# A list-scheduled plan that begins four experts earlier, with the sums of those experts' weights split ahead

## The chip, the cores and the metric

The kernel runs on one core of a Trainium2 chip, as one program of five engines (TensorE, VectorE, ScalarE, GpSimd and SyncE, in the profile PE, DVE, ACT, POOL and SP) that each run their own queue in order and wait for each other on semaphores. The metric is the device time of one execution in microseconds: the median of three runs was 1813.43 us (1811.5 to 1813.5).

## The reference

Four batches of 576 tokens and 8 heads of 64 go through a retention layer (attention scores times a decay, no softmax). The result is 2304 tokens of 512 values. A first mixture of experts sends each token through one of 8 experts, and a second one sends every token through all 8 and adds them with weights `P` from a Sinkhorn iteration:

```
logits = x @ w_gate;  P = exp(logits - logits.max())
for _ in range(8):
    P /= P.sum(1, keepdims=True) + 1e-09
    P /= P.sum(0, keepdims=True) + 1e-09
    P *= N / E
for e in range(E):
    h = np.maximum(x @ w1[e], 0.0)        # 2304x512 @ 512x1024
    out += P[:, e:e+1] * (h @ w2[e])      # 2304x1024 @ 1024x512
```

All is float32. The second mixture is most of the work.

## The kernel before

A float32 matrix is cut into a high half that TensorE takes (`fp32r`) and the rest (`lo_of`, line 236), and a product is three matmuls: high by high, high by low, low by high. ScalarE makes the high half, VectorE the low one.

After retention and the first mixture (from about 98 to 338 us) the second mixture goes over the tokens in 3 passes of 768, and in each pass over 8 experts. The first weights use a scheme of seven products instead of eight, on sums and differences of blocks. A unit is a quarter of an expert's hidden columns: 7 products of 6 matmuls with 384 columns each.

**The hand-written part** is pass 0, 32 units (`unit`, line 1243). Its raw weights come by DMA into 5 raw tiles, and each weight tile is made in four steps (`split_step`, line 239) into one of 4 ring tiles. A "plain" slot is split as it is. A "sums" slot first needs four additions of 128x256 on GpSimd into the one tile `sums`; steps 0 and 1 split loaded blocks, steps 2 and 3 the sums. The steps are dropped at fixed places of a unit: `mid` "a" to "d" and three places of their own. At its start a unit stores its finished sums to HBM (`w1s`), 896 KB for each half, so that the later passes need not make them again. Between its products a unit does the second weights' work of the unit before it in plain form (`second`, line 1179): 36 matmuls of 512 columns. In experts 0 and 1, `gate_step` (line 1326) also runs the Sinkhorn iteration at places "b" and "d", and at its end `weigh` (line 1212) multiplies the six accumulators by `P`, three of them on GpSimd.

**The plan** does passes 1 and 2. Each piece of work is a `Task` with an engine, a duration and what it comes after. TensorE's order is written out (`line0` for the plan's first expert, in which the last hand-written unit's second weights are finished, then `GAPS`); every other engine takes the ready task that is due first, in a simulated run. In the plan the second weights use the scheme of seven products too: 252 matmuls of 256 columns for an expert. Weight sums are read back from `w1s`. The step from one pass to the next is `load_pass` (line 1462).

Of the kernel before, what the change touches and what calls it, by code (L numbers as in the profile page):

```python
# [7 lines left out]
F32 = mybir.dt.float32  # L8
# [28 lines left out]
def kernel(  # L37
# [18 lines left out]
    nc = tc.nc  # L56
    N, DM = out.shape
    E, _, F = w11.shape
# [86 lines left out]
    NP = 3  # L145
    RING = 4
# [18 lines left out]
    SPOTS = "bd"  # L165
    raws, slots, lo_n = [], [], [LO_AT]
# [5 lines left out]
    class Slot:  # L172
        def __init__(self, kind, parts, col=0):
            self.kind, self.parts, self.col = kind, parts, col
            slots.append(self)
            for r in parts:
                raws[r][3] = len(slots)
# [17 lines left out]
    def w2_slots(i):  # L195
        for f in range(2):
            Slot("plain", [part((i, f, r), lambda i, f, r: rows2(expert(w12, i), 2 * f + r))
                           for r in range(2)])

    for i in range(E):  # L200
        w1_slots(i)
        w2_slots(i)
    for p in range(1):
        for e in range(E):
            for j in range(2):
                pr = [part((e, j, h), lambda e, j, h: w21[e][:, h * half + 256 * j:h * half + 256 * (j + 1)]
                           .rearrange("(k p) f -> p k f", p=128)) for h in range(2)]
                Slot("sums", pr, 0)
                Slot("sums", pr, 128)
                Slot("plain", [part((e, j, h), lambda e, j, h: rows2(w22[e], 2 * h + j)) for h in range(2)])  # L210
    n_load, n_split, n_rel, n_take, n_known = [0], [0], [0], [0], [0]
# [12 lines left out]
    def load_more():  # L224
        while n_load[0] < n_known[0]:
            n = n_load[0]
            if n >= RAW and raws[n - RAW][3] * 4 > n_split[0]:
                return
            key, make, _, _ = raws[n]
            ap = make(*key)  # L230
            t = raws[n][2] = rawt[n % RAW]
            raws[n].append(arrives(1.46))
            nc.sync.dma_start(out=t.rearrange("p (k f) -> p k f", f=ap.shape[2]), in_=ap)
            n_load[0] += 1
# [4 lines left out]
    def split_step(n=1, force=False):  # L239
        for _ in range(n):  # L240
            load_more()
            j, s = divmod(n_split[0], 4)
            if j >= min(len(slots), n_rel[0] + RING):
                return
# [7 lines left out]
            if s == 0:  # L252
                c.hi, c.lo = (ringt[j % RING][:, 2048 * n:2048 * (n + 1)] for n in range(2))
# [11 lines left out]
            else:  # L265
                fa, fb = (raws[r][2].rearrange("p (k f) -> p k f", k=4)[:, :, c.col:c.col + 128] for r in c.parts)
# [14 lines left out]
            n_split[0] += 1  # L281
        load_more()

# [3 lines left out]
    def take():  # L287
        j = n_take[0]
# [4 lines left out]
        n_take[0] += 1  # L293
        return slots[j]

    def release(n=1):
        n_rel[0] += n
# [945 lines left out]
    def unit(u, pre, mids):  # L1243
# [3 lines left out]
        for k, x in enumerate((w.hi, w.lo)):  # L1247
            nc.sync.dma_start(out=w1s[4 * u["e"] + u["i"]][:, k], in_=x[:, 0:1792].bitcast(F32))
        arrives(5.2)
# [14 lines left out]
        def renew(j):  # L1264

            if u["last"]:
                xsplit(j)
# [11 lines left out]
        renew(0)  # L1279
# [7 lines left out]
        renew(1)  # L1287
# [4 lines left out]
        renew(2)  # L1292
# [6 lines left out]
        renew(3)  # L1299
# [6 lines left out]
        renew(4)  # L1306
# [5 lines left out]
        renew(5)  # L1312
# [5 lines left out]
        renew(6)  # L1318
# [29 lines left out]
    n_unit = E * 4  # L1348
    for g in range(n_unit):
# [3 lines left out]
             "last": e == E - 1 and i == 3 and p + 1 < NP}  # L1353
# [4 lines left out]
        elif g == 1:  # L1358
            mids = {k: (lambda _, n=n: gate_step(5 + n)) for n, k in enumerate(("p0", "p1", "p2"))}
            for k in "bcd":  # L1360
                mids[k] = gate_step
        elif p == 0 and e < 2 and gate_queue:
            mids = {k: gate_step for k in SPOTS}
        elif p + 1 < NP and e == E - 3 and i == 3:
            mids = {k: (lambda b, n=n: xload(p + 1, n)) for n, k in enumerate("bc")}
        elif p + 1 < NP and e == E - 2 and i > 1:
            mids = {"b": lambda b, n=i - 2: xsums(n)}
# [72 lines left out]
    JORD = {s: (0, 1, 2, 5, 3, 4, 6) if s < n_exp - 1 else (0, 1, 5, 6, 2, 3, 4) for s in range(E, n_exp)}  # L1440
# [74 lines left out]
    for s in range(E, n_exp):  # L1515
# [3 lines left out]
        for i in range(4):  # L1519
# [9 lines left out]
            where = {"x": 2 * (i % 2) if s == E else 0, "y": 1, "y5": 3 if s == E and i else 1}  # L1529
# [45 lines left out]
            product(0, [prev["x"] if s > E else prev.get(i % 2), tail[-1] if s == E and i else None])  # L1575
# [10 lines left out]
            product(5, [a0 if s > E or i == 0 else prev["y5"]])  # L1586
# [6 lines left out]
            prev["y"], prev["y5"] = a0 if s == E and i else a1, a1  # L1593
            if s == E:
# [3 lines left out]
        if s == E:  # L1598
# [120 lines left out]
        for j in JORD[s]:  # L1719
            for kh in range(2):  # L1720
                for t in range(HB):
                    so, bo = sops[j, kh], bops[j, kh]
                    dep = [so[1], so[2], bo[1], bo[2]]
                    if kh == 0:
# [3 lines left out]
                        else:  # L1728
                            dep += [last_ev[back, t]] if s > E else early_banks
# [17 lines left out]
    for s in range(E + 1, n_exp + 1):  # L1747
# [220 lines left out]
```

## Time and profile before

| what | value |
|---|---|
| median of 3 runs | 1813.43 us |
| profiled execution | 1811.14 us |
| its span | 1809.4 us, granted clock 0.999 |
| TensorE matmul busy | 1785.6 us, 99% |
| VectorE, ScalarE, GpSimd busy | 69%, 49%, 23% |
| DMA | 325.29 MB, mean 180 GB/s |
| first product of pass 0, of the plan | 337.7 us, 841.7 us |

The share of busy time is an average over stages, and matmuls are pipelined, so what a stage is worth is read from the distance of two starts in it. Whether a wait counts is read from whether TensorE stood still for it.

### The profile page before, as it was taken

To read this page: it belongs to the slowest core of one execution; us is meant where nothing else is said; L and a number is where in the kernel's file an instruction comes from. 1 tells how busy PE (TensorE), PEld (TensorE's weight loads), DVE (VectorE), ACT (ScalarE), POOL (GpSimd) and SP (SyncE) were. 2 spreads that over 40 slices of the span, in tenths; PEclk is the share of its full clock that TensorE was granted. 3 is DMA by queue.
4 is the path that set the end of the run, shared out by engine and by line. 5 is a ranking of instruction groups with operands and counts; after the bars stand their busy time and mean duration, and the time that the engine had idled before them with its cause. 6 is when DMAs were issued, how large, how long until landed. Compare 5 with 4: busy or idle time off the path is not lost.

```text
span 1809.4 us, 32670 instructions
## 1 busy us (share of the span) xinstructions
PE 1785.6 (99%) x12398; PEld 1705.3 (94%) x12398; DVE 1244.2 (69%) x2205; ACT 891.4 (49%) x1718; POOL 409.4 (23%) x396
## 2 busy tenths in 40 slices
PE   8999999999999999999999999999999999999998
PEld 7889999998999999998999999999999999999997
DVE  6764666557555655664667787787877777777777
ACT  2454455534443333343565555555656555555553
POOL 4630121221321212213221111111222112111212
PEclk9999999999999999999999999999999999999999
DMA  9854655564545556545755556555555555555540
GB/s 325 298 196 158 213 184 190 186 217 155 197 176 192 192 192 227 185 164 188 234 155 169 158 163 191 166 163 153 150 182 181 162 164 153 177 160 156 155 129 36
DMA packets 190597, 325.29 MB, mean 180 GB/s; under 512 B 20551, under 2 KB 93400, under 8 KB 190429
## 3 DMA queue, kind: packets, MB, share of 16 engines
q1 hardware_dynamic: 187132, 312.89, 53.2%
q0 software_dynamic: 3136, 9.95, 1.6%
q8 instruction: 100, 1.64, 0.4%
q14 instruction: 69, 0.56, 0.1%
q10 hardware_dynamic: 160, 0.26, 0.0%
HBM read 248.26 MB, written 74.79 MB: 179 GB/s over the span
## 4 chain that ended last, share of the span: by engine, by line
PE 86%; DVE 3%; issue 2%; ACT 1%; POOL 0%; POOLq 0%; DVEq 0%; ACTq 0%
PE b L1543 8%; PE b L1545 8%; PE b L1544 8%; PE b L1692 8%; PE b L1691 8%; PE b L1690 8%; PE b L1190 5%; PE b L1192 5%; PE b L1191 5%; PE b L1260 4%; PE b L1261 4%; PE b L1262 4%; PE b L722 4%; PE b L724 3%; PE b L723 3%
## 5 line engine op out<-in xcount | busy, mean ns | idle before, releaser
L1691 PE MATMUL b<-wb,sq 128*128 128x256 f32 x1344 | 378.5, 282 | 1.1 <-DVE wb L237 1.1
L1690 PE MATMUL b<-wb,sq 128*128 128x256 f32 x1344 | 377.1, 281 | 0.9 <-DVE a L1712 0.9
L1692 PE MATMUL b<-wb,sq 128*128 128x256 f32 x1344 | 377.1, 281 | 0.4 <-DVE sq L237 0.4
L1691 PEld LDWEIGHTS b<-wb,sq 128*128 128x128 f32 x1344 | 254.0, 189 | 1.7 <-DVE wb L237 1.7
L1692 PEld LDWEIGHTS b<-wb,sq 128*128 128x128 f32 x1344 | 254.4, 189 | 0.6 <-DVE sq L237 0.6
L1690 PEld LDWEIGHTS b<-wb,sq 128*128 128x128 f32 x1344 | 252.9, 188 | 1.8 <-issue 1.3
L237 DVE TENSOR_TENSOR ring<-raw,ring 128x512 fp32r<-128x512 f32 (+1 forms) x256 | 192.5, 761 | 69.2 <-ACT ring L260 61.0
L237 DVE TENSOR_TENSOR sq<-hq,sq 128x768 fp32r<-128x768 f32 x167 | 168.8, 1015 | 68.3 <-ACT sq L1636 68.2
L1448 POOL TENSOR_TENSOR raw<-raw,raw 128x512 f32<-128x512 f32 x60 | 84.8, 1414 | 384.2 <-DVE wb L237 313.3
L1558 ACT ACTIVATE hq<-hq 128x384 f32<-128x384 f32 x144 | 75.6, 526 | 184.4 <-DVE hq L1555 183.7
L1543 PE MATMUL b<-ch,wa 128*128 128x384 f32 x448 | 151.4, 338 | 2.2 <-DVE hq L1555 1.6
L1260 PE MATMUL b<-ch,ring 128*128 128x384 f32 x448 | 152.5, 340 | 0.2
L1543 PE MATMUL b<-c,wa 128*128 128x384 f32 x448 | 151.2, 337 | 1.1 <-ACT u L1549 1.1
L1636 ACT CAST sq<-hq 128x768 fp32r<-128x768 f32 x167 | 137.6, 829 | 29.2 <-PE b L1691 24.5
L1545 PE MATMUL b<-ch,wa 128*128 128x384 f32 x448 | 150.6, 336 | 0.0
L1545 PE MATMUL b<-c,wa 128*128 128x384 f32 x448 | 150.6, 336 | 0.0
L1261 PE MATMUL b<-cl,ring 128*128 128x384 f32 x448 | 150.6, 336 | 0.0
L1262 PE MATMUL b<-ch,ring 128*128 128x384 f32 x448 | 150.6, 336 | 0.0
L1544 PE MATMUL b<-cl,wa 128*128 128x384 f32 x448 | 150.6, 336 | 0.0
L1544 PE MATMUL b<-c,wa 128*128 128x384 f32 x448 | 150.5, 336 | 0.0
L1190 PE MATMUL b<-ring,HH 128*128 128x512 f32 x384 | 149.8, 390 | 0.0
L1192 PE MATMUL b<-ring,HL 128*128 128x512 f32 x384 | 149.5, 389 | 0.0
(258 smaller groups left out, 4179.5 us busy)
## 6 DMA issues: line engine op xcount, KB each, us to landing
wa<-w1s SPq DMA_DIRECT2D x192, 512.0 KB, 4.2
raw<-in_moe_w_dram SPq DMA_DIRECT2D x128, 512.0 KB, 3.9
w1s<-ring SPq DMA_DIRECT2D x64, 896.0 KB, 5.9
raw<-in_moe_w_dram SPq DMA_DIRECT2D x106, 256.0 KB, 3.5
wa<-w1s SPq DMA_DIRECT2D x64, 256.0 KB
sums<-in_moe_w_dram SPq DMA_DIRECT2D x22, 256.0 KB, 3.2
xs<-x SPq DMA_DIRECT2D x19, 256.0 KB, 4.8
kT<-in_kT_dram SPq DMA_DIRECT2D x18, 256.0 KB, 4.0
```

The costliest lines, as they stand in the source:

```text
L237: eng.tensor_tensor(lo, x, hi.bitcast(F32), ALU.subtract)
L1190: nc.tensor.matmul(y[t], hh[:, s], w.hi[:, f0:f0 + 512], start=first, stop=False)
L1192: nc.tensor.matmul(y[t], hl[:, s], w.hi[:, f0:f0 + 512], start=False, stop=end)
L1260: nc.tensor.matmul(ps, a, xh[:, r, :], start=first and r == 0, stop=False, skip_group_check=True)
L1261: nc.tensor.matmul(ps, a, xl[:, r, :], start=False, stop=False, skip_group_check=True)
L1262: nc.tensor.matmul(ps, b, xh[:, r, :], start=False, stop=r == 1, skip_group_check=True)
L1543: nc.tensor.matmul(ps, a, xh[:, r, :], start=first, stop=False, skip_group_check=True)
L1544: nc.tensor.matmul(ps, a, xl_[:, r, :], start=False, stop=False, skip_group_check=True)
L1545: nc.tensor.matmul(ps, b, xh[:, r, :], start=False, stop=r == 1, skip_group_check=True)
L1690: nc.tensor.matmul(ps, hh[:, r, c], wh[:, r], start=st, stop=False, skip_group_check=True)
L1691: nc.tensor.matmul(ps, hh[:, r, c], wl[:, r], start=False, stop=False, skip_group_check=True)
L1692: nc.tensor.matmul(ps, hl[:, r, c], wh[:, r], start=False, stop=kh == 1 and r == 1, skip_group_check=True)
```

## The change

The plan begins at expert 4 of pass 0 (`S0 = 4`), after 16 hand-written units instead of 32. What the plan needs from HBM for experts 4 to 7, their 16 tiles of sums, is made ahead: an extra "sums" slot with a `store` number loads one 128-column block of each half (two DMAs into one raw tile), goes through the same four steps into a ring tile, is stored to `w1s`, and its ring tile is free at once. Six such slots stand in the first mixture (`MADE_IN`), ten in experts 0 to 3. Ring tiles are handed out by a list of free ones. The places in a unit call `keep_up`, which does two steps where the splits are behind. The last unit no longer prepares the next pass, so both changes of pass are the plan's.

```
+    S0 = 4
+    MADE_IN = (0, 1, 1, 1, 1, 1, 1, 0)
+    made = [(e, i) for e in range(S0, E) for i in range(4)]
+    def make_ahead():
+        e, i = made.pop(0)
...
+        def source(e, i, _):
+            return [w21[e][:, h * half + 128 * i:h * half + 128 * (i + 1)].rearrange("(k p) f -> p k f", p=128)
+                    for h in range(2)]
+        Slot("sums", [part((e, i, 0), source)], 0, store=4 * e + i)
     for i in range(E):
         w1_slots(i)
-        w2_slots(i)
+        for _ in range(MADE_IN[i]):
+            make_ahead()
+        for f in range(2):
+            w2_slot(i, f)
...
+    for e in range(S0):
+        for j in range(2):
+            pr = sum_parts(e, j)
+            for col in (0, 128):
+                if made and (j or e in (1, 2) and col):
+                    make_ahead()
+                Slot("sums", pr, col)
...
-            if j >= min(len(slots), n_rel[0] + RING):
+            if j >= len(slots) or (s == 0 and not ring_free):
                 return
...
+                c.ring = ring_free.pop(0)
...
             n_split[0] += 1
+            if s == 3 and c.store is not None:
+                store_sums(c, c.store)
+                ring_free.append(c.ring)
...
         def mid(k, free):
...
             if free is not None:
-                split_step()
+                keep_up()
...
-    n_unit = E * 4
+    n_unit = S0 * 4
...
-        elif p + 1 < NP and e == E - 3 and i == 3:
-            mids = {k: (lambda b, n=n: xload(p + 1, n)) for n, k in enumerate("bc")}
...
-    for s in range(E, n_exp):
+    for s in range(S0, n_exp):
```

ScalarE's queue where expert 0 ends and expert 1 begins. `ring` is a ring tile, `c` a kept product or a hidden sum, `HH` the hidden tile's high half, `b0` a PSUM bank. Before:

```order
L1238 COPY c_6525<-b0_6482 128x384 [waits PE_49]
L279 CAST ring2_80<-sums_84 128x512 [waits Pool_49]
L1238 COPY c_6554<-b0_6482 128x384 [waits PE_49,Activation_49]
L279 CAST ring2_80<-sums_84 128x512 [waits Pool_49]
L1233 ACTIVATE HH_111<-b0_6482 128x384 [waits PE_49,Activation_49]
L279 CAST ring3_71<-raw2_65 128x512 [waits DMAHW0_49]
L1228 ACTIVATE HH_111<-c_6588 128x384 [waits DVE_49,Activation_49]
L279 CAST ring3_71<-raw3_66 128x256
L1228 ACTIVATE HH_111<-c_6619 128x384 [waits DVE_49,Activation_49]
L279 CAST ring3_71<-sums_84 128x512 [waits Pool_49]
```

and now:

```order
L1278 COPY c_6656<-b0_6611 128x384 [waits PE_49,Activation_49]
L308 CAST ring2_80<-sums_84 128x512 [waits Pool_49]
L308 CAST ring0_78<-raw2_65 128x512 [waits DMAHW2_49,DMAHW1_49]
L1278 COPY c_6691<-b0_6611 128x384 [waits PE_49,Activation_49]
L308 CAST ring0_78<-raw2_65 128x256 [waits DMAHW2_49]
L308 CAST ring0_78<-sums_84 128x512 [waits Pool_49]
L1273 ACTIVATE HH_111<-b0_6611 128x384 [waits PE_49,Activation_49]
L308 CAST ring0_78<-sums_84 128x512 [waits Pool_49]
L1268 ACTIVATE HH_111<-c_6725 128x384 [waits DVE_49,Activation_49]
L308 CAST ring0_78<-raw0_63 128x512 [waits DMAHW7_49,Activation_49]
L1268 ACTIVATE HH_111<-c_6760 128x384 [waits DVE_49]
```

A whole made-ahead slot (`ring0`) now stands between the last step of one sums slot and the first of the next, the copy of its sums ahead of the activation `HH<-b0`; and the slot after it begins in the same `ring0` (lane DMAHW7 is that of the store).

ScalarE's queue in the fourth unit of expert 1. Before:

```order
L279 CAST ring0_78<-raw0_63 128x512 [waits DMAHW3_49]
L1228 ACTIVATE HH_111<-c_7096 128x384 [waits DVE_49,Activation_49]
L279 CAST ring0_78<-raw1_64 128x256 [waits DMAHW0_49]
L1238 COPY c_7108<-b0_7065 128x384 [waits PE_49,Activation_49]
L279 CAST ring0_78<-sums_84 128x512 [waits Pool_49]
L1238 COPY c_7127<-b0_7065 128x384 [waits PE_49,Activation_49]
```

and now:

```order
L308 CAST ring1_79<-raw1_64 128x512 [waits DMAHW3_49]
L308 CAST ring1_79<-raw2_65 128x256 [waits DMAHW4_49]
L1268 ACTIVATE HH_111<-c_7275 128x384 [waits DVE_49,Activation_49]
L308 CAST ring1_79<-sums_84 128x512 [waits Pool_49]
L1278 COPY c_7287<-b0_7242 128x384 [waits PE_49,Activation_49]
L308 CAST ring1_79<-sums_84 128x512 [waits Pool_49]
L308 CAST ring2_80<-raw3_66 128x512 [waits DMAHW6_49,DMAHW5_49]
L1278 COPY c_7312<-b0_7242 128x384 [waits PE_49,Activation_49]
```

The copy of the sums has moved ahead of the first kept product (`c_7287`), and a step of the next slot stands ahead of the second.

GpSimd's queue at the start of the plan (`out_0_dram` is a scatter of finished rows, `raw` the second weights' blocks). Before:

```order
L237 TENSOR_TENSOR cl_10152<-x_9126,ch_10151 128x768 [waits Activation_49]
L112 DMA out_0_dram<-a0_6673,idc_2052 2304x512 [waits DMAHW5_49,DVE_49]
...
L112 DMA out_0_dram<-a4_6747,idc_2052 2304x512 [waits DVE_49]
L1448 TENSOR_TENSOR raw3_66<-raw2_65 128x512 [waits DMAHW7_49,DMAHW6_49]
L1448 TENSOR_TENSOR raw2_65<-raw2_65,raw0_63 128x512 [waits DMAHW2_49,Pool_49]
...
L112 DMA out_0_dram<-a5_6752,idc_2052 2304x512 [waits DMASW7_49,DVE_49]
```

and now:

```order
L300 TENSOR_TENSOR sums_84<-raw1_64,sums_84 128x256 [waits Pool_49]
L1470 TENSOR_TENSOR raw3_66<-raw2_65 128x512 [waits DMAHW3_49,DMAHW2_49]
L1470 TENSOR_TENSOR raw2_65<-raw2_65,raw0_63 128x512 [waits DMAHW6_49,DMAHW5_49,Pool_49]
L1473 TENSOR_TENSOR raw0_63<-raw3_66,raw0_63 128x512 [waits DVE_49,Pool_49]
L1470 TENSOR_TENSOR raw1_64<-raw1_64,raw0_63 128x512 [waits DMAHW0_49,DVE_49,Pool_49]
```

The scatters, and the split `cl` of the next pass's tokens, no longer stand ahead of the plan's first sums.

## Rows read from the trace of the kernel before

**Rows 1.** Windows: PE, PEld, DVE, ACT, POOL busy us, granted clock, DMA share, GB/s.
```profile
594.00:656.00 62.00, 62.00 (x314) 56.16 (x313) 35.94 (x59) 24.69 (x52) 12.15 (x16) 1.00 0.52 187
941.00:1000.00 59.00, 59.00 (x423) 59.00 (x422) 45.05 (x70) 31.61 (x56) 10.37 (x8) 1.00 0.54 161
406.00:422.30 16.30, 16.21 (x83) 14.43 (x83) 13.28 (x32) 9.03 (x19) 3.63 (x4) 1.00 0.38 106
501.10:516.50 15.40, 15.40 (x79) 13.99 (x78) 8.64 (x14) 6.38 (x13) 3.20 (x4) 1.00 0.36 114
```

**Rows 2.** Timeline of PE: start us, duration; first matmuls of experts.
```profile
593.95 0.34 PE L1260 MATMUL b<-ch,ring 128*128 128x384 f32 x1
...
655.88 0.34 PE L1260 MATMUL b<-ch,ring 128*128 128x384 f32 x1
...
841.66 0.34 PE L1543 MATMUL b<-ch,wa 128*128 128x384 f32 x1
...
882.28 0.34 PE L1543 MATMUL b<-ch,wa 128*128 128x384 f32 x1
...
941.21 0.34 PE L1543 MATMUL b<-ch,wa 128*128 128x384 f32 x1
...
1000.15 0.34 PE L1543 MATMUL b<-ch,wa 128*128 128x384 f32 x1
...
1295.04 0.34 PE L1543 MATMUL b<-c,wa 128*128 128x384 f32 x1
...
1356.41 0.34 PE L1543 MATMUL b<-c,wa 128*128 128x384 f32 x1
```

**Rows 3.** Start of the plan: waits (total, times, longest us), then DVE and POOL timelines.
```profile
PE b L1543 <- DVE hq L1555: 1.6, 2, 1.0
...
859.01 3.10 DVE L237 TENSOR_TENSOR wb<-raw,wb 128x512 fp32r<-128x512 f32 x3
...
857.93 1.32 POOL L1448 TENSOR_TENSOR raw<-raw 128x512 f32<-128x512 f32 x1
```

**Rows 4.** Fourth unit of expert 0: timelines of DVE, POOL, ACT and PE.
```profile
399.88 1.29 DVE L237 TENSOR_TENSOR ring<-sums,ring 128x512 fp32r<-128x512 f32 x2
...
403.98 0.55 DVE L1226 TENSOR_TENSOR c<-b,c 128x384 f32<-128x384 f32 x1
...
401.25 0.74 POOL L272 TENSOR_TENSOR sums<-raw 128x256 f32<-128x256 f32 x1 [21.95 <-DVE ring L237]
...
401.86 0.49 ACT L1233 ACTIVATE HH<-b 128x384 fp32r<-128x384 f32 x1 [2.09 <-PE b L1262]
...
404.83 0.42 PE L1260 MATMUL b<-ch,ring 128*128 128x384 f32 x1
...
409.10 0.34 PE L1260 MATMUL b<-ch,ring 128*128 128x384 f32 x1
```

**Rows 5.** DMA, 607 to 617 us: GB/s in 40 slices; issues, KB, us to landing.
```profile
GB/s 33 0 0 0 0 41 49 147 180 279 295 225 254 279 438 496 446 430 459 459 459 430 430 402 315 430 401 401 459 459 459 229 86 0 0 0 0 0 0 0
...
w1s<-ring SPq DMA_DIRECT2D x2, 896.0 KB, 5.9
```

**Rows 6.** Fourth unit of expert 1: timelines of POOL, ACT and PE.
```profile
454.71 4.67 POOL L1218 TENSOR_SCALAR a<-a,P 128x512 f32<-128x512 f32 x3 [17.77 <-issue]
...
461.29 0.91 POOL L271 TENSOR_TENSOR sums<-raw,raw 128x256 f32<-128x256 f32 x1
...
460.33 0.47 ACT L1238 COPY c<-b 128x384 f32<-128x384 f32 x1
...
461.12 0.39 PE L1190 MATMUL b<-ring,HH 128*128 128x512 f32 x1
...
461.80 0.34 PE L1260 MATMUL b<-ch,ring 128*128 128x384 f32 x1
...
462.15 0.34 PE L1262 MATMUL b<-ch,ring 128*128 128x384 f32 x1
```

**Rows 7.** First mixture: timelines of DVE and POOL.
```profile
243.90 1.92 DVE L237 TENSOR_TENSOR ring<-raw,ring 128x512 fp32r<-128x512 f32 x1 [0.77 <-ACT ring L260]
...
243.43 1.83 POOL L237 TENSOR_TENSOR cl<-x,ch 128x768 fp32r<-128x768 f32 x1 [13.11 <-ACT ch L1075]
```

More of the change, by code (lines that the diff above doesn't have):

```diff
@@ L145 @@
     NP = 3
-    RING = 4
     GAT0 = 14
@@ L172, with __init__ @@
     class Slot:
-        def __init__(self, kind, parts, col=0):
-            self.kind, self.parts, self.col = kind, parts, col
+        def __init__(self, kind, parts, col=0, store=None):
+            self.kind, self.parts, self.col, self.store = kind, parts, col, store
+            self.ring = None
             slots.append(self)
@@ L252, in split_step @@
             if s == 0:
-                c.hi, c.lo = (ringt[j % RING][:, 2048 * n:2048 * (n + 1)] for n in range(2))
+                c.ring = ring_free.pop(0)
+                c.hi, c.lo = (ringt[c.ring][:, 2048 * n:2048 * (n + 1)] for n in range(2))
             if c.kind == "plain":
@@ L265, in split_step @@
             else:
-                fa, fb = (raws[r][2].rearrange("p (k f) -> p k f", k=4)[:, :, c.col:c.col + 128] for r in c.parts)
+                if c.store is None:
+                    fa, fb = (raws[r][2].rearrange("p (k f) -> p k f", k=4)[:, :, c.col:c.col + 128] for r in c.parts)
+                else:
+                    both = raws[c.parts[0]][2].rearrange("p (h k f) -> p h k f", h=2, k=4)
+                    fa, fb = (both[:, h] for h in range(2))
                 hi = c.hi.rearrange("p (j f) -> p j f", f=128)
@@ L281, in split_step, with store_sums @@
             n_split[0] += 1
+            if s == 3 and c.store is not None:
+                store_sums(c, c.store)
+                ring_free.append(c.ring)
         load_more()
+    def store_sums(c, n):
+        for k, x in enumerate((c.hi, c.lo)):
+            nc.sync.dma_start(out=w1s[n][:, k], in_=x[:, 0:1792].bitcast(F32))
+        arrives(5.2)
     def keep_up():
@@ L287, in take @@
     def take():
+        while slots[n_take[0]].store is not None:
+            n_take[0] += 1
         j = n_take[0]
@@ L293, in take, with release @@
         n_take[0] += 1
+        held.append(slots[j])
         return slots[j]
-    def release(n=1):
-        n_rel[0] += n
+    def release():
+        ring_free.append(held.pop(0).ring)
     tiles = _tiles()
@@ L1246, in unit @@
         w = take()
-        for k, x in enumerate((w.hi, w.lo)):
-            nc.sync.dma_start(out=w1s[4 * u["e"] + u["i"]][:, k], in_=x[:, 0:1792].bitcast(F32))
-        arrives(5.2)
+        store_sums(w, 4 * u["e"] + u["i"])
         if u["i"] % 2:
@@ L1311, in unit @@
         h_sum(u, 3, yb, u3)
-        renew(5)
         if pre:
@@ L1352 @@
         u = {"p": p, "e": e, "i": i, "h": {}, "y": {} if i == 0 else pre["y"], "w2": None,
-             "last": e == E - 1 and i == 3 and p + 1 < NP}
+             }
         mids = {}
@@ L1527 @@
             P_, made = {}, {}
-            where = {"x": 2 * (i % 2) if s == E else 0, "y": 1, "y5": 3 if s == E and i else 1}
+            where = {"x": 2 * (i % 2) if s == S0 else 0, "y": 1, "y5": 3 if s == S0 and i else 1}
             def chunk(j, wg=wg, bank_t=bank_t, where=where):
@@ L1746 @@
     b, owed = [], 0
-    for s in range(E + 1, n_exp + 1):
+    for s in range(S0 + 1, n_exp + 1):
         b += [g2[s - 1, j, kh, t] for j in JORD[s - 1] for kh in range(2) for t in range(HB)]
```

54 lines of the change are left out of this document (22 added, 32 removed).

## The prediction

> **What bounds the kernel now.** I read the windows of busy time first. An expert of the first pass's hand-written part and an expert of the plan both show TensorE busy in every microsecond, at a granted clock of 1.00 (the 2.4 GHz level), while VectorE is busy 35.9 of 62 us and 45.1 of 59 us, ScalarE 24.7 and 31.6 [rows 1]. So the time is the number of matmuls in each style, plus the places where TensorE waits. Next come the starts of experts on TensorE [rows 2]: two experts of the hand-written part start at 593.95 and 655.88, 61.93 us apart; two of the plan at 941.21 and 1000.15, 58.94 us apart. Both do 168 matmuls of 384 columns for the first weights; for the second weights the one does 144 of 512 columns, the other 252 of 256. Then I looked for what is not at this pace: the start of the plan, a pass change inside it, and the Sinkhorn steps in experts 0 and 1, where VectorE is busy 13.3 of 16.3 us against 8.6 of 15.4 in an ordinary unit [rows 1].
>
> **The change part by part.** The sum is made against the profiled execution: 1811.14 us, span 1809.4, and 2.3 us under the median of 1813.43.
>
> *Four experts move into the plan.* 4 x (61.93 - 58.94) = 12.0 us less [rows 2]. Nothing covers TensorE there, so this counts in full.
>
> *The start of the plan*, now after expert 3. Before, it takes from 841.66 to 882.28, 40.6 us [rows 2]. Its content is 168 matmuls of 384 columns, 0.174 us apart, and 36 of 512 columns, 0.227 us apart [rows 6], which is 29.2 + 8.2 = 37.4 us: 3.2 us are waits. Two of these waits, 1.6 us together, end with VectorE's addition for the hidden tile [rows 3]; VectorE is late because three weight subtractions took 3.10 us while GpSimd was doing its own sums [rows 3], against 0.65 us for such a subtraction alone (two in 1.29 us, [rows 4]). GpSimd does these sums late because scatters of the finished pass stand ahead of them in its queue. At expert 3 no pass ends, so the scatters are not there, and the sums can run earlier, beside idle stretches of VectorE. I take 0.8 us less; bounds: 1.6 us less if both waits go, 0.5 us more if the sums meet another VectorE operation.
>
> *A pass change inside the plan.* The change from pass 0 to pass 1 used to be made by hand in the last unit; it is now made by the plan, as the one from pass 1 to 2 is. That one takes 61.37 us from 1295.04 to 1356.41 [rows 2], 2.4 us over the pace. I add 2.4 us; bounds 1.5 and 4. Gain so far: 12.0 + 0.8 - 2.4 = 10.4 us.
>
> *Sixteen sums made ahead.* The work is the same as before for ScalarE, VectorE, GpSimd and the stores; it is moved from experts 4 to 7, six pieces into the first MoE and ten into experts 0 to 3 (2, 3, 3, 2). Each piece is 4 ScalarE copies, 4 VectorE subtractions, 4 GpSimd additions, two loads and two stores of 896 KB. On the average this fits: three pieces add some 3 x 4 x 0.65 = 7.8 us to VectorE's 36 of 62. What counts is the queues, since every engine runs in order. Where a critical operation must be done before TensorE's next product, a piece ahead of it can push it over. I went through the units in the changed order; three places are tight.
>
> First, the fourth unit of expert 0. Before, VectorE finishes the Sinkhorn step and then splits two pieces at 399.88 (1.29 us), GpSimd starts the next additions at 401.25, and ScalarE's activation comes at 401.86 [rows 4]. Now the last subtraction of one piece stands right before the first of a made-ahead piece, and there is one buffer for sums: GpSimd starts its additions at 400.6, three of them take 2.2 us (0.74 each), and ScalarE, whose copy of these sums now stands ahead of the activation, gets to it at 403.5 instead of 401.86. VectorE's subtractions and its addition follow (0.65, 0.55, 0.65 and 0.55 us): the addition ends at 406.0, where the one of before started at 403.98 and the product that needs it at 404.83 [rows 4]. Wait: 1.2 us.
>
> Second, the same ring buffer. This piece's store is issued at about 404.8 (high half) and 405.5 (low half), and the next piece takes the same buffer at once: ScalarE and VectorE wait for the store. A pair lands 5.9 us after its issue [rows 5]: 410.6. The queued subtraction (0.7) and the next addition (0.55) end at 411.9; the product that needs it starts at 409.10 before [rows 4], now 410.35: 1.5 us. ScalarE's copy for the product after that comes late too, by no more than it did before. The bounds of this store wait: nothing if the pair lands within 4.2 us, 2.6 us if other transfers stand before it. I take 1.4. Together 2.6 us.
>
> By the Trainium skill, DMA: Bandwidth & Descriptors, Specifications, one core has about 358 GB/s to HBM; the pair would then move for 5.1 us. The trace disagrees: slices of this stretch run at 430 to 459 GB/s [rows 5], and the pair moves in about 4.3 us. By the rule both store waits would be 0.8 us longer.
>
> Third, the second unit of expert 1 has the same two pieces back to back behind a Sinkhorn step: 1.2 us again, and its last Sinkhorn step is then late by 0.5 us: 1.7 us. Fourth unit of expert 1: GpSimd weights the accumulators for 4.67 us from 454.71, and the third addition after it ends at 462.2 [rows 6]. Before, ScalarE's copy for the next product stands ahead of the copy that waits for these sums, and is done at 460.8; the product starts at 461.80 [rows 6]. Now the order is the other way round: sums copy 462.25 to 462.87, then the 0.47 us copy, product at 463.3: 1.5 us. At the end of this unit the piece after the made-ahead one takes the same buffer again: 1.3 us more (I reckon 0 to 2.6 again). 2.8 us. Smaller shifts of VectorE in the other Sinkhorn units (a subtraction of 512 columns where one of 256 stood): 0.6 us. Bill of the hand-written part: 2.6 + 1.7 + 2.8 + 0.6 = 7.7 us; bounds 1 and 14.
>
> In the first MoE the six pieces fall into 16 slots per expert that had room: the second weights' part has only evictions to make, and three of the four doubled steps lie there. VectorE's subtractions are stretched where GpSimd works beside them: 1.92 us while GpSimd has one of 1.83 us [rows 7]. I take 0.3 us; bounds 0 and 9 (below).
>
> *Sum:* 1811.14 - 10.4 + 7.7 + 0.3 = 1808.7 for the profiled execution; with 2.3 us for the median, **1811.0 us**.
>
> **The rivals.** *The queues have the room* (28%). For it: everywhere outside the Sinkhorn units VectorE idles seven of 15.4 us [rows 1], and a delay of one operation in a unit need not reach TensorE. Against it: the buffer taken at once is there in the order, whatever the averages. If the store lands in time and the sums come early, some 1 to 2 us of the 8 remain: 1813.4 - 10.4 + 1.5 = 1804.5.
>
> *Slower: VectorE and GpSimd meet in the first MoE* (13%). If the additions of a made-ahead piece run in the first weights' part of an expert, beside the subtraction that frees a bank, each of the six pieces costs what the rows of one such meeting show: 1.92 - 0.65 = 1.3 us [rows 4, 7], and with the split that stands behind it some 1.7 us. Six times that is 10 us instead of 0.3: 1811 + 10 = 1821. It decides from 5.9 us of such waits on (the 2.4 us forecast and 3.6 more). Against it: the copies of a piece stand where the bank has no reader waiting, and its loads are issued well ahead, so that the additions run in the second weights' part.
>
> The Trainium skill, SBUF - State Buffer, "SBUF: two separate sides", says that GpSimd and a VectorE operation with two operands in SBUF exclude each other for a whole instruction. The trace agrees in kind (1.92 us here is 0.65 plus most of one GpSimd operation). By the rule each of the 64 GpSimd operations that are moved can hold VectorE for its whole 0.74 us; if one in four stands on the path, that is 12 us, which is this rival's size.
>
> *The plan does less than it says* (14%). If the start keeps its 3.2 us of waits and the pass change out of pass 0, with less lead for its loads, costs 4 us, the gain is 8 us, and the bill of 8 eats it: 1813.4, no change.
>
> **How the numbers follow.** Forecast 45%, with a range of its own from 1808.5 to 1813.5; the rivals 28, 13 and 14%. What can be told from no change is about 0.2%, 3.6 us: faster is under 1809.8, slower over 1817.0. Faster: all of the first rival and a third of the forecast, 0.43. Slower: 0.13. Between: 0.44. Range: 1803.5 (gain whole, almost no bill) to 1817.5, which leaves out most of the slow rival and a little at the fast end.
>
> **What would show it.** In the changed profile: experts 4 to 7 at 58.9 us each; a start of the plan of about 40 us and a pass change of about 61.4; on TensorE, waits of 1 to 2 us in the fourth units of experts 0 and 1 and the second of expert 1, put down to VectorE's hidden-tile addition or ScalarE's copy, and on ScalarE and VectorE behind them waits for a DMA at the ring's casts. No such waits would make the first rival right. Units of the first MoE longer by over 1 us each would make the second right. The forecast is wrong if experts 4 to 7 are not at the plan's pace, or if TensorE waits in experts 2 and 3, where I reckon with nothing.

## The result and the profile after

The changed kernel took 1828.0 us (median of 4 runs, 1824.6 to 1828.5), the kernel before 1813.5 beside it: 1.0078 times as long, 95% interval 1.006 to 1.0095. The forecast of 1811.0 and its range (to 1817.5) were wrong, and so was the sign; "slower" had 13%, for meetings in the first mixture that did not come. The profiled execution took 1827.6 us, span 1825.5.

First the starts of experts, PE's timeline of the changed kernel (start us, duration, in brackets the idle time before and what ended it); they answer to [rows 2].

```profile
342.19 0.34 PE L1298 MATMUL b<-ch,ring 128*128 128x384 f32 x1
...
617.68 0.69 PE L1565 MATMUL b<-ch,wa 128*128 128x384 f32 x1 [4.18 <-DMA wa<-w1s]
...
660.38 0.34 PE L1565 MATMUL b<-ch,wa 128*128 128x384 f32 x1
...
719.31 0.34 PE L1565 MATMUL b<-ch,wa 128*128 128x384 f32 x1
...
837.42 0.34 PE L1565 MATMUL b<-c,wa 128*128 128x384 f32 x1
...
898.78 0.34 PE L1565 MATMUL b<-c,wa 128*128 128x384 f32 x1
```

An expert of the plan takes 58.93 us (660.38 to 719.31), the change into pass 1 61.36: as forecast. Experts 0 to 3 took 275.5 us (342.19 to 617.68) where they took 256.25 before, and the plan starts with a wait of 4.18 us for its first weights. The windows of the changed kernel, in the columns of [rows 1], are an expert of the plan and the fourth units of experts 0 and 1:

```profile
660.40:719.30 58.90, 58.90 (x421) 58.90 (x420) 44.06 (x68) 30.27 (x54) 7.89 (x7) 1.00 0.63 197
...
468.30:487.80 19.50, 16.27 (x80) 13.83 (x79) 12.63 (x18) 10.38 (x21) 13.85 (x14) 1.00 0.61 222
396.60:416.10 19.50, 17.02 (x84) 14.32 (x83) 15.04 (x33) 8.69 (x19) 8.94 (x11) 1.00 0.61 235
```

TensorE is busy 16.3 and 17.0 of 19.5 us in these units, where [rows 1] has 16.2 of 16.3 in another unit with a Sinkhorn step, the first of expert 1. What it waits for, 345 to 490 us of the changed kernel (total, times, longest us):

```profile
PE b L1298 <- ACT c L1278: 4.2, 5, 2.2
PE b L1298 <- DVE c L1266: 3.6, 5, 1.3
PE b L1207 <- DVE HL L1274: 0.8, 2, 0.4
PE b L1298 <- DVE cr L1208: 0.6, 2, 0.3
```

These are the waits that the prediction named, for ScalarE's kept product and VectorE's hidden tile. The table has the us that each unit takes, from its first matmul on PE to the next unit's: before, after, and four of the experiments below. (0,3) is the fourth unit of expert 0.

| unit | before | after | e1 | e5 | e4 | e11 |
|---|---|---|---|---|---|---|
| (0,1) | 16.67 | 18.24 | 16.69 | 16.67 | 16.67 | 16.67 |
| (0,2) | 16.10 | 16.61 | 17.66 | 16.32 | 16.48 | 17.12 |
| (0,3) | 15.94 | 19.49 | 19.99 | 17.56 | 17.57 | 18.62 |
| (1,0) | 16.35 | 17.13 | 17.09 | 16.48 | 16.51 | 17.98 |
| (1,1) | 15.93 | 17.93 | 17.94 | 17.57 | 17.57 | 15.93 |
| (1,2) | 16.34 | 17.11 | 17.11 | 16.10 | 16.14 | 15.93 |
| (1,3) | 15.50 | 19.53 | 21.17 | 16.60 | 16.60 | 21.15 |
| (2,0) | 15.47 | 16.95 | 16.91 | 15.47 | 15.47 | 16.89 |
| (2,1) to (2,3) | 46.47 | 46.74 | 46.67 | 46.41 | 47.27 | 46.52 |
| (3,0) to (3,2) | 46.44 | 46.41 | 46.41 | 46.41 | 50.21 | 46.41 |
| (3,3) | 15.50 | 19.81 | 15.47 | 15.47 | 15.47 | 15.47 |
| plan's first expert | 40.62 | 42.70 | 40.59 | 40.97 | 40.32 | 40.31 |

The last matmul starts 16.1 us later than before, from these parts: the first unit starts 4.5 us later; units (0,1) to (3,2) take 14.9 more; (3,3), with the wait behind it, 4.3; the plan's first expert 2.1; the change into pass 1 2.7 (2.4 in its own expert, 0.25 in the one ahead of it); experts moved into the plan take off 12.0; 0.4 less elsewhere.

### The profile page after: what moved, and what is told of

Read it like the earlier page. It is cut to its first block, busy times and chain, and to the rows that moved or that the text cites. A ratio compares the mean times of both kernels' runs of the same rounds, so it can differ in the third digit from the quotient of the medians.

```text
span 1825.5 us, 34067 instructions
## 1 busy us (share of the span) xinstructions
PE 1782.6 (98%) x12830; PEld 1719.8 (94%) x12830; DVE 1323.2 (72%) x2320; ACT 949.0 (52%) x1798; POOL 455.9 (25%) x421
## 4 chain that ended last, share of the span: by engine, by line
PE 78%; DVE 5%; issue 4%; DMA 2%; POOL 1%; ACT 1%; POOLq 0%; SPq 0%; DVEq 0%; ACTq 0%
PE b L1565 10%; PE b L1567 10%; PE b L1566 10%; PE b L1714 10%; PE b L1713 10%; PE b L1712 10%; PE b L762 4%; PE b L764 3%; PE b L763 3%; PE b L1230 1%; PE b L1298 1%; PE b L1231 1%; PE b L1232 1%; PE b L1300 1%; PE b L1299 1%
## 5 line engine op out<-in xcount | busy, mean ns | idle before, releaser
L1713 PE MATMUL b<-wb,sq 128*128 128x256 f32 x1680 | 473.0, 282 | 1.1 <-DVE wb L261 1.1
L1714 PE MATMUL b<-wb,sq 128*128 128x256 f32 x1680 | 471.4, 281 | 0.8 <-DVE sq L261 0.8
L1712 PE MATMUL b<-wb,sq 128*128 128x256 f32 x1680 | 471.2, 280 | 0.9 <-DVE a L1734 0.9
L1714 PEld LDWEIGHTS b<-wb,sq 128*128 128x128 f32 x1680 | 318.0, 189 | 1.2 <-DVE sq L261 1.2
L1713 PEld LDWEIGHTS b<-wb,sq 128*128 128x128 f32 x1680 | 317.5, 189 | 1.7 <-DVE wb L261 1.7
L1712 PEld LDWEIGHTS b<-wb,sq 128*128 128x128 f32 x1680 | 316.1, 188 | 1.8 <-issue 1.3
L1565 PE MATMUL b<-c,wa 128*128 128x384 f32 x896 | 302.4, 337 | 2.0 <-ACT u L1571 2.0
L1567 PE MATMUL b<-c,wa 128*128 128x384 f32 x896 | 301.3, 336 | 0.0
L1566 PE MATMUL b<-c,wa 128*128 128x384 f32 x896 | 301.1, 336 | 0.0
L261 DVE TENSOR_TENSOR sq<-hq,sq 128x768 fp32r<-128x768 f32 x208 | 207.3, 1000 | 81.0 <-ACT sq L1658 80.9
L1734 DVE SCALAR_TENSOR_TENSOR a<-b,P,a 128x256 f32<-128x256 f32 x306 | 141.1, 476 | 49.7 <-PE b L1714 48.9
L261 DVE TENSOR_TENSOR wb<-raw,wb 128x512 fp32r<-128x512 f32 x231 | 163.1, 708 | 19.0 <-ACT wb L1658 19.0
L1565 PEld LDWEIGHTS b<-c,wa 128*128 128x128 f32 x896 | 169.1, 189 | 2.9 <-ACT u L1571 2.8
L1567 PEld LDWEIGHTS b<-c,wa 128*128 128x128 f32 x896 | 168.4, 188 | 0.0
L1566 PEld LDWEIGHTS b<-c,wa 128*128 128x128 f32 x896 | 168.3, 188 | 0.0
L1658 ACT CAST wb<-raw 128x512 fp32r<-128x512 f32 x231 | 142.6, 618 | 46.1 <-PE b L1714 44.5
L1571 ACT COPY u<-b 128x384 f32<-128x384 f32 x160 | 76.3, 477 | 74.1 <-PE b L1567 73.6
L285 ACT CAST ring<-raw 128x512 fp32r<-128x512 f32 x160 | 95.3, 619 | 9.0 <-DMA raw<-in_moe_w_dram 7.8
```

The lines of the kernel that those rows point to most:

```text
L261: eng.tensor_tensor(lo, x, hi.bitcast(F32), ALU.subtract)
L285: nc.scalar.copy(c.hi[:, o:o + 512], x[:, i:i + 512])
L1565: nc.tensor.matmul(ps, a, xh[:, r, :], start=first, stop=False, skip_group_check=True)
L1566: nc.tensor.matmul(ps, a, xl_[:, r, :], start=False, stop=False, skip_group_check=True)
L1567: nc.tensor.matmul(ps, b, xh[:, r, :], start=False, stop=r == 1, skip_group_check=True)
L1658: nc.scalar.copy(o.tile[0], src.tile)
```

## The experiments

In each the ratio is to the kernel before, run beside it (1810.9 us for e1 to e4, 1812.1 for e5 to e8, 1812.0 for e9 to e12).

### The place of the plan's first weights: e1

SyncE's timeline of the changed kernel shows the loads of these weights going out at 613.53 us, 4.2 us ahead of the matmul at 617.68; of SyncE's wait ahead of them, 14.2 us are put down to the last product of unit (3,3) (PE b L1300, last row: SyncE's waits, 594 to 620 us). The weights go into memory that had been a ring tile, and that tile was the one unit (3,3) was multiplying from.

```profile
591.94 1.05 SPq L318 DMA_DIRECT2D w1s<-ring  x2
613.53 3.25 SPq L1532 DMA_DIRECT2D wa<-w1s  x5
...
SPq L1532 <- PE b L1300: 14.2, 1, 14.2
```

```
-    ring_free, held = list(range(4)), []
+    ring_free, held = [0, 2, 1, 3], []
```

> The changed kernel (1828.0 us) with two of the four ring tiles exchanged (free list begins 0, 2, 1, 3 instead of 0, 1, 2, 3); nothing else differs. Theory, the place in memory: the plan's first weights are loaded into memory that the last hand-written unit still multiplies from, so their load is issued only at that unit's last product (613.5 us) and TensorE waits 4.2 us. With the exchange that ring tile is another one, the load goes out some 14 us earlier, the wait of 4.2 us is gone: 1823.8 us. Rival, the transfers: the load is late because stores and raw loads stand before it in the queue; then the wait stays and the time is 1828.

Measured: 1820.7 us, 1.0052 (1.0034 to 1.0069). The same view of e1: the loads begin at 595.48, and the first matmul follows the last unit without a gap.

```profile
590.40 1.05 SPq L318 DMA_DIRECT2D w1s<-ring  x2
595.48 17.68 SPq L1532 DMA_DIRECT2D wa<-w1s  x5
```

So the place in memory was the cause. In the traces (3,3) and the plan's first expert together go from 62.5 to 56.1 us, more than the wait: the 2.1 us on top were a lower clock (below). The ratios differ by 0.26%, 4.7 us; e1's profile has a fall of the clock of its own in (1,3).

### The sums buffer and the stores: e2, e3, e8

e2 gives GpSimd a third half-buffer:

```
+    sumx = sum_p.tile([128, 512], F32, name="sums2")
...
-                    z = c.sums = sumt.rearrange("p (j f) -> p j f", f=128)
+                    y = sumt[:, 0:512].rearrange("p (j f) -> p j f", f=128)
+                    z = (sumt[:, 512:1024], sumx)[n_sum[0] % 2].rearrange("p (j f) -> p j f", f=128)
...
```

> The changed kernel with the sums buffer widened from two halves to three (512 more columns), so that GpSimd can begin the sums of the next slot while VectorE still reads those of the last one. Theory, one sums buffer: in the units (0,3), (1,1) and (1,3) ScalarE stands 3.8, 3.8 and 1.8 us before a copy of sums that GpSimd began late because VectorE still held the buffer, and the kept product and the hidden tile queue behind it; these units lose 9.5 us and about half of that goes: 1823 us. Rival, the store holds the ring tile: the wait only moves from the sums to the tile, 1827.5. Rival, too much work in one unit (VectorE, ScalarE and GpSimd together): no gain over 0.5 us, 1827.5 to 1828.

Measured: 1823.6 us, 1.0071 (1.0054 to 1.0088), some 1.3 us less than the changed kernel by the ratios. ScalarE's waits for sums fell from 11.7 us to 0.2 (waits of ScalarE, units (0,1) to (2,1)), yet the units (0,1) to (2,3) only from 189.7 to 188.4 us (186.8 without a fall of the clock in (1,3), 1.6 us, that the changed kernel's profile doesn't have). The wait is real, and worth some 1 to 3 us by the traces.

e3 lets a ring tile rest after its store:

```
+            while resting and (force and not ring_free or resting[0][0] <= clock["pe"]):
+                ring_free.append(resting.pop(0)[1])
...
-                ring_free.append(c.ring)
+                resting.append((clock["pe"] + 6, c.ring))
```

> The changed kernel with a ring tile of a made-ahead piece given back 6 us (in the planner's count) after its store instead of at once, so that no split is written into a tile whose store is on its way. Theory, the store holds the ring tile: VectorE waited 2.0 and 2.9 us and ScalarE 1.7 and 1.7 us for stores in the units around (0,1), (0,3), (1,3) and (2,0), of which 3 to 5 us reach TensorE: 1824 us. Theory, the sums buffer and the order of the queues: the same chain is late for another reason, 1827 to 1829. Since the tiles change their turn, the last unit's weights also stand in another tile here, which by itself takes off the 4.2 us of the plan's first weights; both figures are then 4.2 us lower, 1820 and 1824.

Measured: 1819.8 us, 1.0051 (1.0034 to 1.0068). That is e1, and nothing beside it: (0,1) to (2,3) take 191.2 us in both. The waits of VectorE and ScalarE for stores fell from 9.4 to 4.7 us in this stretch, and on the whole TensorE gained nothing from it. That does not rule the stores out. In the changed kernel three of TensorE's waits stand behind VectorE's addition, and that addition behind a subtraction that waited for a store. VectorE's and PE's timelines of the changed kernel in (0,1) and (2,0):

```profile
377.61 0.69 DVE L261 TENSOR_TENSOR ring<-raw,ring 128x512 fp32r<-128x512 f32 x1 [1.99 <-DMA w1s<-ring]
378.83 0.44 PE L1298 MATMUL b<-ch,ring 128*128 128x384 f32 x1 [1.30 <-DVE c L1266]
...
490.74 0.69 DVE L261 TENSOR_TENSOR ring<-raw,ring 128x512 fp32r<-128x512 f32 x1 [2.86 <-DMA w1s<-ring]
491.95 0.45 PE L1298 MATMUL b<-ch,ring 128*128 128x384 f32 x1 [0.93 <-DVE c L1266]
```

With 0.57 us in (1,0) these are 2.8 us. In e1 the same three waits stand in (0,2), (1,0) and (2,0); e3 takes 3.2 us less in these units, and 3.2 us more in (1,1) and (2,1) to (2,3), where one such wait (2.38 us of VectorE, ahead of a wait of 0.43 us of TensorE in (2,2)) stands again. The rest moved the loss and did not remove it; more ring tiles, which would test the store by itself, were not run.

e8 joins e1 and e2.

> The changed kernel with both the exchanged ring tiles and the sums buffer of three halves, all sixteen pieces where the change puts them. Theory: the two gains add, 4.4 us and some 3 us that the experts 0 to 3 took less with the wider buffer: 1817 to 1818 against 1825 for the changed kernel on this chip. Rival, with the wider buffer the next queue is late and nothing is left of the gain: 1820.5.

Measured: 1817.2 us, 1.0025 (1.0015 to 1.0035): the two add. By the ratios it is 9.6 us under the changed kernel, where e1 and e2 alone gave 4.7 and 1.3, each to within some 4 us; the traces' gains are 3.2 us over e1 (1.6 of them a fall of the clock that this profile does not have). (0,1) to (2,3) take 188.0 us, still 13 over before.

### Pieces, or doubled steps: e4, e5

e4 has no piece in experts 0 and 1.

```
-    MADE_IN = (0, 1, 1, 1, 1, 1, 1, 0)
+    MADE_IN = (1, 1, 1, 1, 1, 1, 1, 1)
...
-                if made and (j or e in (1, 2) and col):
+                if made and (e, j, col // 128) in {(e, j, n) for e in (2, 3) for j in (0, 1) for n in (0, 1)}:
```

> The changed kernel with no made-ahead piece in experts 0 and 1: one piece in each of the eight experts of the first mixture, four in expert 2 and four in expert 3. Theory, the pieces meet the Sinkhorn steps: units (0,1) to (2,0) lost 14.7 us against the kernel before, which all goes, the last unit's weights stand in another ring tile (4.2 us less), and a fourth piece in experts 2 and 3 costs 0 to 1.5 us each: 1808 to 1812. Rival, a piece costs its 1.5 us wherever it stands: the eight in experts 2 and 3 lose 8 us there and the time is 1817 to 1820. Rival, the loss is of the new slot order and not of the pieces: 1824.

Measured: 1821.7 us, 1.0057 (1.004 to 1.0074), far over the 1808 to 1812 expected. Of the 14.7 us that (0,1) to (2,0) had lost, 10 went. New losses took the gain's place: four pieces in expert 3 cost 3.8 us there, and in this profile (0,0) starts 7.9 us later than before, 2.04 of them a wait for a split at its first matmul, and takes 2.2 us longer, the clock falling behind that wait. Both stand behind the piece in the last expert of the first mixture, which no other run has. But the table also shows that (0,3), (1,1) and (1,3) stay 1.1 to 1.6 us over before, *without a piece in them*. One line of the change is left in these units: inside a unit, the four places "a" to "d" of `mid`, which took one split step, take two when the planner is behind (the expectations of e5, e6 and e9 count three). e5 is the kernel before with that line alone:

```
             if free is not None:
-                split_step()
+                keep_up()
```

> The kernel before with one line of the change alone: the three places inside a unit that take one split step take two when the planner is behind. No sums are made ahead and the plan still begins at the second pass. Theory, doubled steps bunch the splits beside the Sinkhorn steps: the units (0,3), (1,1) and (1,3) take 17.6, 17.6 and 16.6 us as they did in the run without pieces in experts 0 and 1, against 15.9, 15.9 and 15.5, and the time is 4.3 us over the kernel before, 1815. Rival, it is the extra slots and the order of the ring, not the doubling: no change, 1811.

Measured: 1817.9 us, 1.003 (1.0018 to 1.0042). The same three units, at the same 17.56, 17.57 and 16.60 us: 4.4 us over before for (0,1) to (2,3); the rest of the 5.7 us is not in these units (in the profile 2.3 came ahead of them, in the first mixture, where the clock fell once). Timelines of GpSimd, ScalarE and PE in unit (0,3) of e5:

```profile
403.18 1.12 POOL L272 TENSOR_TENSOR sums<-raw 128x256 f32<-128x256 f32 x1 [20.78 <-DVE ring L237]
404.37 0.81 POOL L271 TENSOR_TENSOR sums<-sums,raw 128x256 f32<-128x256 f32 x1
...
405.90 0.62 ACT L279 CAST ring<-sums 128x512 fp32r<-128x512 f32 x1 [3.81 <-POOL sums L271]
406.43 0.49 ACT L1233 ACTIVATE HH<-b 128x384 fp32r<-128x384 f32 x1
...
408.84 0.45 PE L1260 MATMUL b<-ch,ring 128*128 128x384 f32 x1 [0.68 <-DVE c L1226]
```

This is the chain that the prediction reckoned for the made-ahead piece (sums, copy, activation, addition), made here by an ordinary split that the doubling pulled forward.

### Are the doubled steps to blame for all: e9

e9 is the changed kernel with that line taken back, all sixteen pieces in place.

> The changed kernel with the doubled steps taken back: the three places inside a unit take one split step, as before the change, with all sixteen pieces where the change puts them. Theory: the doubling alone costs 4.4 us in experts 0 and 1, and goes; but a unit then takes fewer steps than its slots need, the rest is forced at the start of a unit, where TensorE waits for it: four such starts (the slots of second weights) with 3 to 4 us each, so 1822 to 1832, no gain on the whole. The last unit's weights stand in another ring tile, which takes off 4.4 us as in the first of these runs. Rival, the steps find their place without the doubling: 1816.

Measured: 1826.2 us, 1.0075 (1.0059 to 1.009). As expected the splits then fall behind and are forced where a unit takes its second weights; PE's timeline of e9 in (0,3) and (1,3):

```profile
393.38 0.75 PE L1230 MATMUL b<-ring,HH 128*128 128x512 f32 x1 [2.98 <-ACT ring L285]
...
466.94 0.80 PE L1230 MATMUL b<-ring,HH 128*128 128x512 f32 x1 [4.45 <-ACT ring L285]
```

Two more such waits, of 1.81 us, stand in (2,3) and (3,3), and the granted clock fell behind each of the four. Against e1, whose plan starts as smoothly, e9 is some 4 us slower by the ratios: with ten more slots in these experts the doubling is one price of the pieces, not an oversight beside them.

### What of a piece costs: e10, e11

Both have e1's ring order, and leave a part of the ten pieces of experts 0 to 3 (store numbers from 22 on) undone: e10 GpSimd's sums (first two lines), e11 VectorE's subtractions (last two).

```
+                    if c.store is None or c.store < 22:
                         sub = lambda o, a, b: nc.gpsimd.tensor_tensor(o, a, b, ALU.subtract)
...
+                if c.store is None or c.store < 22:
                     lo_of(nc.vector, lo[:, o:o + n_], x, hi[:, o:o + n_])
```

> With the exchanged ring tiles, and the ten pieces made in experts 0 to 3 without their four GpSimd operations each (their sums are left out, the copies, subtractions, loads and stores stay). The units (0,1) to (2,3) take 191.2 us with the exchanged tiles alone and 179.2 with the doubling but no pieces: 12 us are the pieces', 1.6 of them a lower granted clock after a stall. Theory, GpSimd beside VectorE: the sums make VectorE's subtractions 1.1 us long instead of 0.65 and hold the one sums buffer; without them 7 to 10 of the 12 us go, 1811 to 1814. Theory, VectorE's and ScalarE's own queues: at most 3 go, 1818.

> With the exchanged ring tiles, and the ten pieces made in experts 0 to 3 without their four VectorE subtractions each (the lower parts are left out; sums, copies, loads and stores stay). Theory, VectorE's own queue: the 40 subtractions of 0.65 to 1.1 us stand before the additions for the hidden tile; without them 7 to 10 of the 12 us go, 1811 to 1814. Theory, GpSimd's sums and the one buffer: at most 5 go, as the buffer also comes free sooner, 1816 to 1818.

Measured: e10 1815.6 us, 1.0019 (1.001 to 1.0029); e11 1814.3, 1.0011 (1.0002 to 1.0021). By the traces (0,1) to (2,3) take 188.7 and 186.8 us against e1's 191.2, so 2.5 and 4.4 of the 12 us go; by the medians 6 and 7 us of the whole (e1's interval alone is some 6 us wide). e10's theory falls by the traces, which are with its rival (at most 3), and is missed by the median, which lies between the two; e11 comes to the near end of its own by the medians and to half of it by the traces. So the operations of a piece are part of its price, and not the whole. What is left shows in (1,3), which neither touches. Timelines of the changed kernel there: VectorE, GpSimd, ScalarE, PE.

```profile
472.94 4.46 DVE L261 TENSOR_TENSOR ring<-raw,ring 128x512 fp32r<-128x512 f32 x4
477.33 0.55 DVE L1266 TENSOR_TENSOR c<-b,c 128x384 f32<-128x384 f32 x1
...
468.32 4.67 POOL L1258 TENSOR_SCALAR a<-a,P 128x512 f32<-128x512 f32 x3 [6.88 <-DVE P L1210]
...
474.79 1.20 POOL L300 TENSOR_TENSOR sums<-raw,raw 128x256 f32<-128x256 f32 x1
...
478.90 0.47 ACT L1278 COPY c<-b 128x384 f32<-128x384 f32 x1
...
479.43 0.44 PE L1298 MATMUL b<-ch,ring 128*128 128x384 f32 x1 [2.19 <-ACT c L1278]
```

The same four subtractions by shape (count, busy us, mean ns), from the changed kernel's groups between 472.9 and 477.3 us:

```profile
L261 DVE TENSOR_TENSOR ring<-raw,ring 128x512 fp32r<-128x512 f32 x3 | 3.6, 1248 | 0.0
L261 DVE TENSOR_TENSOR ring<-raw,ring 128x256 fp32r<-128x256 f32 x1 | 0.9, 949 | 0.0
```

Four subtractions stand together ahead of the addition of the hidden tile; ScalarE's activation waits for that addition, its kept product stands behind the activation, and TensorE waits for the kept product. All four belong to *ordinary* slots: with the additions of a piece gone (e10) or its subtractions (e11) they still stand there, as the same two views of e11 show:

```profile
465.24 4.47 DVE L261 TENSOR_TENSOR ring<-raw,ring 128x512 fp32r<-128x512 f32 x4
...
471.73 0.45 PE L1299 MATMUL b<-ch,ring 128*128 128x384 f32 x1 [2.23 <-ACT c L1279]
```

Before, one subtraction stood at this place, and in e5 two, the second of 256 columns (VectorE's timelines, before first):

```profile
457.87 1.18 DVE L237 TENSOR_TENSOR ring<-raw,ring 128x512 fp32r<-128x512 f32 x1 [0.33 <-ACT ring L279]
458.97 0.54 DVE L1226 TENSOR_TENSOR c<-b,c 128x384 f32<-128x384 f32 x1
...
463.39 1.52 DVE L237 TENSOR_TENSOR ring<-raw,ring 128x512 fp32r<-128x512 f32 x2 [0.32 <-ACT ring L279]
464.83 0.54 DVE L1226 TENSOR_TENSOR c<-b,c 128x384 f32<-128x384 f32 x1
```

The likely reason, read from the order and not tested by itself: a piece makes the slots behind it late, lateness doubles the steps, and the doubled steps come in a row. Beside GpSimd's additions a subtraction of 512 columns takes 1.25 us, not the 0.65 of [rows 4]. By the Trainium skill, SBUF — State Buffer, "SBUF: two separate sides", a GpSimd operation and a VectorE one with two operands in SBUF hold the shared port in turn for whole instructions; these rows agree in kind, though 0.6 us more for each is less than the 0.7 to 1.2 us of one GpSimd operation here.

### A version without these places: e6, e7, e12

The plan begins at expert 5, so twelve pieces: six in the first mixture, two each in experts 2 to 4; single steps in experts 0 and 1. With the plan begun there, the last unit's weights come to stand in a tile that the plan's first load does not need.

```
-    S0 = 4
+    S0 = 5
...
-                if made and (j or e in (1, 2) and col):
+                if made and (e, j, col // 128) in {(e, 1, n) for e in (2, 3, 4) for n in (0, 1)}:
...
-                keep_up()
+                keep_up() if u["e"] > 1 else split_step()
```

> A version for both causes: the plan begins at expert 5, so twelve sums are made ahead, six in the first mixture, two in each of the experts 2, 3 and 4, none in experts 0 and 1, where a unit's three places take one split step again. The last hand-written unit's weights stand in a ring tile that the plan's first weights don't need. Theory: experts 0 and 1 take what they took before, the start of the plan too (40.6 us), three experts save 2.99 us each, the pass change made by the plan costs 2.7: 1811 - 9.0 + 2.7 = 1804.7 us. Rival, a piece in an expert costs some 1.5 us wherever it stands: 1804.7 + 9 = 1813.7. Rival, the first mixture loses to its six pieces: 3 us more.

Measured: 1808.2 us, 0.9976 (0.9967 to 0.9986): 3.9 us faster than the kernel before, where 6.3 were expected. Experts 0 and 1 take what they took before. Missing are 1.0 us in (2,3) and 2.7 at the start of the plan (657.42 to 700.76, 43.3 us), part of it a wait behind VectorE's addition and the clock that fell after it, in PE's timeline of e6:

```profile
683.68 0.60 PE L1565 MATMUL b<-ch,wa 128*128 128x384 f32 x1 [1.91 <-DVE hq L1577]
```

e7 is e6 with e2's third half-buffer.

> The same, with the sums buffer of three halves. Theory, where no unit has both a piece and a Sinkhorn step the sums buffer is no bound: 0 to 1 us less than the last, 1804 to 1805. Rival, what is left in experts 2 to 4 is the sums buffer: 2 to 3 us less.

Measured: 1808.5 us, 0.9978 (0.9968 to 0.9989): no gain over e6, as the theory had it; the level is e6's.

e12 is e6 with the six pieces in other slots, and the free list begun 0, 3, 2, 1.

> The version that begins the plan at expert 5, with its six pieces of the hand-written experts placed one in expert 2, three in expert 3 and two in expert 4 instead of two in each. Theory: the 1.0 us that the unit (2,3) lost and the waits of 1.2 us at the start of the plan hang on where the pieces stand; 1 to 2 us less than the version with two in each, 1806.5. Rival, expert 3 now loses what expert 2 did: 1808.

Measured: 1811.4 us, 0.9996 (0.9987 to 1.0005): 3 us worse than e6. (2,2) takes 1.5 us more and (3,0) 1.6, and the start of the plan is no better (43.35 us). In both units TensorE waits behind VectorE's addition (0.91 and 1.05 us), and VectorE's timeline of e12 shows what it stood behind:

```profile
504.79 0.69 DVE L261 TENSOR_TENSOR ring<-raw,ring 128x512 fp32r<-128x512 f32 x1 [3.03 <-DMA w1s<-ring]
...
537.33 0.69 DVE L261 TENSOR_TENSOR ring<-raw,ring 128x512 fp32r<-128x512 f32 x1 [3.17 <-DMA w1s<-ring]
```

It is the wait for the store again. The theory falls; the rival had the direction, and the loss is larger than it said.

## Why the prediction was wrong, point by point

- *Four experts at the plan's pace, 12.0 us*: right (3.00 us each).
- *Pass change in the plan, 2.4 us*: right (2.7).
- *First MoE, 0.3 us*: not contradicted, and not measured closely. In the eleven profiles with the same six pieces the first unit of pass 0 starts between 336.9 and 342.2 us, in the middle at 338.75; before it was 337.7, and in e5, without pieces, 340.0. So most of the 4.5 us is this execution's own: 2.3 were there before the first piece, where the order of instructions is the kernel before's, and 2.0 were a stall of 1.90 us instead of 1.46 and the fall of the clock after it. The rival of six meetings at 1.7 us each did not happen.
- *Start of the plan, -0.8 us*: **this step failed**. It looked at GpSimd's scatters and VectorE's addition, and those waits are nearly what they were (1.4 us against 1.6 in [rows 3]). What it did not ask is which ring tile the last unit holds, and what the plan puts there: 4.2 us of wait and 2.1 of clock, all of it gone in e1, which then takes 40.6 us, as before. The wait stands in SyncE's queue; the prediction went through VectorE, ScalarE, GpSimd and the stores, not this load.
- *Bill of the hand-written part, 7.7 us*: **this step failed too**; the kinds of wait were right, and the sum has half the size (14.9). By its own terms: the sums and their copy in (0,3) 1.2 us, measured 3.6; the store behind it, which falls in (1,0), 1.4, measured 0.8; (1,1) 1.7, measured 2.0; (1,3) 1.5, measured 4.0; the store behind that, in (2,0), 1.3, measured 1.5; all other units 0.6, measured 3.1, of which 1.6 are a third store wait, in (0,1). The store terms were thus about right where they stood, and one was missing; the term of one sums buffer (2.4 us) measures 1 to 3. Too small by 4.9 us together are (0,3) and (1,3). Missing there was the doubled step: the sum priced each made-ahead piece where it stands, and not the ordinary splits that the doubling moves beside the Sinkhorn steps, 4.4 us with no piece at all (e5: 1.6 in (0,3), 1.6 in (1,1), 1.1 in (1,3)). That the term of (1,1) fits is luck, since that unit loses most of it without a piece. That lateness behind a piece bunches them further is read from (1,3).
- *"The forecast is wrong if TensorE waits in experts 2 and 3"*: it does; (2,0) takes 1.5 us more, and 4.2 us are waited behind (3,3). The store waits at the ring's casts, which it named as its sign, are there too.

What stays open: of the 12 us of the pieces in experts 0 to 2 (e1 against e5) 1.6 are a fall of the clock, some 1 to 3 the sums buffer, some 3 the stores as the traces show them, and up to half the pieces' own operations. These overlap, and the share of bunched ordinary splits is not measured by itself.

## What to carry to other kernels

A planner that catches up in bursts turns extra work into bunches of ordinary work: count what stands ahead of a critical operation after the change, not only what the change adds. When buffers change their turn, look at who inherits the memory of the last one used: a load for the next stage waits for its last reader, and its row stands in the load queue, not on the engines that look tight. A buffer given back at once hands the wait for its store to the next owner, and to whatever stands behind that in the queue. Work made ahead fits only where the queues have gaps at every step: here two pieces in each of the experts 2 to 4 gained 3.9 us, and the same six as one, three and two gained nothing clear.

## What the runs showed of the hardware

A stall of about 2 us can cost a second time. Windows of the changed kernel behind the wait of 4.18 us (columns as in [rows 1]; the granted clock is the third from the end):

```profile
617.00:619.00 2.00, 1.32 (x4) 1.32 (x5) 0.00 (x0) 0.00 (x0) 0.00 (x0) 0.50 1.03 361
619.00:621.00 2.00, 2.00 (x7) 1.76 (x6) 0.00 (x0) 0.48 (x1) 0.00 (x0) 0.50 1.00 333
621.00:623.00 2.00, 2.00 (x8) 1.92 (x7) 0.00 (x0) 0.00 (x0) 0.00 (x0) 0.62 1.03 375
623.00:625.00 2.00, 2.00 (x11) 1.77 (x10) 1.22 (x2) 0.08 (x1) 0.00 (x0) 1.00 1.09 377
```

The granted clock is 0.50, the 1.2 GHz level, for some 5 us, and 7 to 8 matmuls are done in 2 us instead of 11: the plan's first expert takes 42.7 us instead of the 40.6 of e1. It is not the same in every execution: in (1,3) TensorE stood still for 2.19 us in the changed kernel and in e1, the clock stayed at 1.00 in the one (19.53 us for the unit) and fell to 0.51 in the other (21.17 us), 1.6 us for one fall. At the start of the plan in e6 and e7 TensorE waits 1.91 us for VectorE's addition in both; the rows behind that wait, e6 first:

```profile
683.70:687.20 3.50, 3.50 (x11) 3.50 (x12) 0.56 (x1) 1.39 (x3) 3.16 (x3) 0.52 0.84 296
685.50:689.00 3.50, 3.50 (x20) 3.50 (x21) 0.56 (x1) 1.43 (x4) 3.16 (x3) 1.00 0.85 296
```

The plan's first expert takes 43.3 us in e6 and 41.8 in e7. After the 1.46 us that TensorE idles at 140 us in the kernel before it did not fall, and after 1.90 us at this place in the changed kernel it did (0.50 from 145 to 148 us). The Trainium skill, TensorE: Matmul & The Clock Gate, Part 1, has only these two levels of the clock, and the rows agree.
